# Attention with unnormalized weights, transposed reciprocals spread by GpSimd, and PSUM dealt out as four, three and one

## The chip, the core and the metric

One core of a Trainium2 chip. Five engines work side by side, each through its own queue in order: TensorE (PE; its weight loads are listed as PEld), VectorE (DVE), ScalarE (ACT), GpSimd (POOL) and SyncE (SP), which issues the DMAs. TensorE writes to PSUM alone, eight banks of 512 fp32 columns on 128 partitions; GpSimd cannot read PSUM. The metric is the device time of one execution in microseconds; less is better.

## The reference

Attention over 4 x 8 heads of 576 positions and 64 dimensions, with a rotation of q and k, and behind it two feed-forward layers on 2304 tokens of width 512 (inner width 2048):

```python
q_rot, k_rot = rotate(q), rotate(k)
scores = matmul(q_rot, k_rot.T) / sqrt(D)
attn = exp(scores - max(scores))
attn = attn / (sum(attn) + 1e-9)
x = matmul(attn, v)                       # -> (2304, 512)
h = x @ w_in;  x = where(h > 0, h, exp(min(h, 0)) - 1) @ w_out
h = x @ w2_in; x = (h - tanh(h)) @ w2_out
```

## The kernel before, in words

The 32 heads go in 16 pairs p. A pair is cut into nine items: four blocks u of 128 queries, each for head h = 0 and h = 1, and a last item (h is None) that holds the remaining 64 queries of both heads. Item i passes through a pipeline that one loop writes out by hand: in step i it emits, in this order, the maximum of item i (VectorE, `emit_max`), the copies out of PSUM that the last step left (`flush`, VectorE and ScalarE by a fixed turn), the scores of item i + 1 (`emit_s`), the exponential of item i with its sum (`emit_exp`, ScalarE), the reciprocal of item i - 1 and its multiplication into the weights (`emit_norm`, L235, VectorE and then GpSimd), the pieces of the rotation of later pairs that are due (`prep`), the transposes of item i - D (`emit_t`, D = 4), and the matmuls with v that are due (`emit_pv`, PV). The remainder of i by 9 is called the slot here. Each engine takes its work in this order.

Scores are made from split numbers: a rotated q or k is held as a rounded high half and a low half, and DMAs put the halves together (`place`, L167: four DMAs for a pair's k, two for each head, and four for q). `prep` has five pieces: two products with the table of cosines and sines, their sum, the high half (L147, ScalarE) and the low half (L152, VectorE), the latter followed by the DMAs. The k of pair p gets its high half in slot 3 and its low half in slot 4 of pair p - 1 (L328); pairs 1 and 2 have entries of their own. The scores of head 0 of pair p are emitted in slot 8 of pair p - 1, those of head 1 in slot 0.

The weights of two query blocks are transposed by TensorE (`pt`; the last 64 key columns of both heads go into `pr`), copied to SBUF (`aT`, `aTr`) and multiplied with v. The items of a group of two blocks are transposed, and L358 says how many steps later its five chunks follow: 12 matmuls after one step, 8 after three; the last group's 20 after two steps, together with the 8 of the second group. With D = 4 the PV stand in slots 3 (12 matmuls), 5 (28), 8 (12) and 1 (8). The result `o` is rounded to `xh` by ScalarE and the rest `xl` made by VectorE (L264 to L274). PSUM: two score tiles of two banks, two banks for transposes, two for outputs.

The feed-forward part works on blocks of 384 tokens, with `xh` and `xl` as its input and an accumulator `acc`; weights come as 64-bit words and are converted beside the rest (`conv_w`).

Of the kernel before, what the change touches and what calls it, by code (L numbers as in the profile page):

```python
# [23 lines left out]
def attention_elu_tanhshrink(ctx: ExitStack, tc: tile.TileContext, qk, v, w1i, w1o, w2i, w2o, tab, out):  # L24
# [22 lines left out]
    xh = const.tile([128, KC, NTOK], F32R, name="xh")  # L47
    xl = const.tile([128, KC, NTOK], F32R, name="xl")
# [52 lines left out]
    with ExitStack() as actx:  # L101
# [10 lines left out]
        tabs = acst.tile([128, 2, S], F32, name="tabs")  # L112
        zero = acst.tile([128, 64], F32, name="zero")
# [5 lines left out]
        def load_qk(p, x):  # L119
            if p == 1 and x == 0:  # L120
                t = p3.tile([128, 2, S], F32, tag="a", name="t0")
            else:
                t = (p1, p2)[x].tile([128, 2, S], F32, tag=f"t{x}", name=f"t{x}")
            nc.sync.dma_start(out=t, in_=qk[p, :, 2 * x:2 * x + 2, :])
            t_t[p, x] = t
# [6 lines left out]
        def prep(p, x, i):  # L132
            t = t_t[p, x]
            mul = SCALE if p > 0 and x == 0 else 1.0
            if i < 2:
                if p == 0 and x == 0:
                    nc.vector.scalar_tensor_tensor(
                        out=t[:, i, :], in0=t[:, i, :], scalar=SCALE, in1=tabs[:, i, :], op0=ALU.mult, op1=ALU.mult
                    )
                else:  # L140
                    eng = nc.vector if p < 2 and i == 1 else nc.gpsimd
                    eng.tensor_tensor(out=t[:, i, :], in0=t[:, i, :], in1=tabs[:, i, :], op=ALU.mult)  # L142
            elif i == 2:
                nc.vector.tensor_tensor(out=t[:, 0, :], in0=t[:, 0, :], in1=t[:, 1, :], op=ALU.add)  # L144
            elif i == 3:
                hl_t[p, x] = p1.tile([128, 2, S], F32R, tag=f"hl{x}", name=f"hl{x}")
                nc.scalar.mul(hl_t[p, x][:, 0, :], t[:, 0, :], mul)  # L147
# [87 lines left out]
        def emit_norm(i):  # L235
# [13 lines left out]

        ev = [0]  # L250
        late, late_x, late_l = [], [], []
# [4 lines left out]
        def flush():  # L256
            for out_, in_ in late:
                ev[0] += 1
                if ev[0] % 5 in (1, 3):
                    nc.vector.tensor_copy(out_, in_)  # L260
                else:
                    nc.scalar.copy(out_, in_)  # L262
            late.clear()
            for x0, hp, o, n in late_l:  # L264
                nc.vector.tensor_tensor(
                    out=xl[:, hp, x0:x0 + n], in0=o[:, 0:n], in1=xh[:, hp, x0:x0 + n].bitcast(F32),
                    op=ALU.subtract,
                )
            late_l.clear()
            for p, grp, o, n in late_x:  # L270
                b, hp = divmod(p, 4)
                x0 = b * S + 256 * grp
                nc.scalar.copy(out=xh[:, hp, x0:x0 + n], in_=o[:, 0:n])
                late_l.append((x0, hp, o, n))  # L274
            late_x.clear()

        def emit_t(i):
            p, u, h = items[i]
            a = a_t[p, u]
            grp = u // 2  # L280
            if (u % 2 == 0) and h in (0, None):
                if grp < 2:
                    aT_t[p, grp] = (p2.tile([128, 2, 4, 256], F32, tag="aT", name="aT"),
                                    p2.tile([128, 256], F32, tag="aTr", name="aTr"))
                else:
                    aT_t[p, grp] = (p1.tile([128, 2, 4, 64], F32, tag="aT2", name="aT2"),
                                    p1.tile([128, 64], F32, tag="aTr2", name="aTr2"))
            aT, aTr = aT_t[p, grp]
            q0 = 128 * (u % 2)
            pt = ps_t.tile([128, 4, 128], F32, tag="pt", name="pt")  # L290
            for c in range(4):
                c0 = 128 * c + (64 if h == 1 else 0)
                nc.tensor.transpose(pt[:, c, :], a[:, h or 0, c0:c0 + 128], ident)  # L293
            if h is None:
                for hh in range(2):
                    evac(aT[:, hh, :, 0:64], pt[:, :, 64 * hh:64 * hh + 64])
                pr = ps_t.tile([128, 4, 128], F32, tag="pt", name="pr")
                for hh in range(2):
                    sl = slice(64 * hh, 64 * hh + 64)
                    nc.tensor.matmul(out=pr[sl, 0, 0:64], lhsT=a[sl, 0, 512:576], rhs=ident[sl, sl],  # L300
                                     start=True, stop=True)
                evac(aTr[:, 0:64], pr[:, 0, 0:64])
                return
            evac(aT[:, h, :, q0:q0 + 128], pt)
            if h == 1:
                pr = ps_t.tile([128, 4, 128], F32, tag="pt", name="pr")
# [3 lines left out]
        o_t = {}  # L310

        def emit_pv(p, grp, c):
# [3 lines left out]
            if c == 0:  # L316
                o_t[p, grp] = ps_v.tile([128, 256], F32, tag="o", name="o")
            o = o_t[p, grp]
            for h in range(2):
                sl = slice(64 * h, 64 * h + 64)  # L320
                if c < 4:
                    w, m = vt[:, 128 * c + 64 * h:128 * c + 64 * h + 64], aT[:, h, c, 0:n]
                else:
                    w, m = vt[sl, 512:576], aTr[sl, 0:n]
# [4 lines left out]
            o_t.pop((p, grp))  # L329
            if grp == 2:  # L330
                v_t.pop(p)
            late_x.append((p, grp, o, n))

        D = 4
# [4 lines left out]
        early = {1: ((None, 0, 0, 1, 2, 3), (None, 0, 0, 0, 1, 2)), 2: ((2, 4, 5, 7, 7, 8), (4, 7, 9, 11, 12, 13))}  # L339
# [11 lines left out]
        with tc.manual_schedule():  # L351
            for x in range(2):
                t = t_t[0, x] = (p1, p2)[x].tile([128, 2, S], F32, tag=f"t{x}", name=f"t{x}")
# [5 lines left out]
            load_qk(1, 1)  # L359
            load_v(0)  # L360
# [10 lines left out]
            pend = []  # L371
            emit_s(0)
# [4 lines left out]
            for i in range(n + D + 1):  # L377
# [4 lines left out]
                if r == 0 and p % 2 == 0 and p // 2 < len(first_w):  # L382
                    load_w(first_w[p // 2])
# [7 lines left out]
                if 0 <= i - 1 < n:  # L391
                    emit_norm(i - 1)
# [20 lines left out]
            flush()  # L413
# [12 lines left out]
    acc = fcst.tile([128, KC * NTOK], F32, name="acc")  # L426
# [6 lines left out]
    def emit_f1(i):  # L433
# [4 lines left out]
        for c in range(KC):  # L438
            ws = slice(128 * c, 128 * c + 128)
            xs = slice(NB * t, NB * t + NB)  # L440
            for wp, x in ((0, xh), (0, xl), (1, xh)):
                nc.tensor.matmul(out=hp, lhsT=w[:, wp, ws], rhs=x[:, c, xs], start=(m == 0), stop=(m == 3 * KC - 1))  # L442
                m += 1
# [61 lines left out]
    def emit_acc():  # L505
        while y_done:
            l, g, t, ys = y_done.pop()
            for e, y in enumerate(ys):
# [11 lines left out]
                if l == 0:  # L520
                    xs = slice(NB * t, NB * t + NB)
                    nc.scalar.copy(out=xh[:, e, xs], in_=a)
                    nc.gpsimd.tensor_tensor(
                        out=xl[:, e, xs], in0=a, in1=xh[:, e, xs].bitcast(F32), op=ALU.subtract
                    )
# [7 lines left out]
    with tc.manual_schedule():  # L533
# [82 lines left out]
```

## Time and profile before

| | us |
|---|---|
| median of three runs (1137.78 to 1139.23) | 1138.52 |
| the profiled execution | 1137.68 |
| its span, first to last instruction | 1135.9 |
| TensorE busy | 1100.1 |
| VectorE, ScalarE, GpSimd busy | 769.7, 689.3, 647.6 |

The attention part takes the first 325 us. The busy time of TensorE counts overlapping matmuls once, and their ends are modelled: the time from one group's start to the next one's start tells its price better than its duration. An idle time stands in brackets with the engine and line that ended it.

### The profile page before, as it was taken

To read this page: it belongs to the slowest core of one execution; us is meant where nothing else is said; L and a number is where in the kernel's file an instruction comes from. 1 tells how busy PE (TensorE), PEld (TensorE's weight loads), DVE (VectorE), ACT (ScalarE), POOL (GpSimd) and SP (SyncE) were. 2 spreads that over 40 slices of the span, in tenths; PEclk is the share of its full clock that TensorE was granted. 3 is DMA by queue.
4 is the path that set the end of the run, shared out by engine and by line. 5 is a ranking of instruction groups with operands and counts; after the bars stand their busy time and mean duration, and the time that the engine had idled before them with its cause. 6 is when DMAs were issued, how large, how long until landed. Compare 5 with 4: busy or idle time off the path is not lost.

```text
span 1135.9 us, 18496 instructions
## 1 busy us (share of the span) xinstructions
PE 1100.1 (97%) x6656; PEld 983.9 (87%) x6656; DVE 769.7 (68%) x1383; ACT 689.3 (61%) x1479; POOL 647.6 (57%) x585
## 2 busy tenths in 40 slices
PE   2899999999999999999999999999999999999998
PEld 1677777777789999999999999999999999999997
DVE  5998889888743434455445466677768777877665
ACT  3677777777634343333333344688888788877774
POOL 2877888778423333333333366676666666666443
PEclk9999999999999999999999999999999999999999
DMA  7767676766211111111111111111111111110102
GB/s 231 197 193 192 191 182 189 200 195 187 72 38 38 38 38 40 54 38 38 57 38 38 38 50 44 38 38 38 56 38 38 38 55 39 38 38 1 57 34 79
DMA packets 29627, 91.96 MB, mean 81 GB/s; under 512 B 4192, under 2 KB 4192, under 8 KB 29536
## 3 DMA queue, kind: packets, MB, share of 16 engines
q1 hardware_dynamic: 29536, 90.78, 27.8%
q8 instruction: 53, 0.87, 0.3%
q14 instruction: 38, 0.31, 0.1%
HBM read 57.74 MB, written 4.72 MB: 55 GB/s over the span
## 4 chain that ended last, share of the span: by engine, by line
PE 86%; DVE 10%; DMA 2%; ACT 1%; issue 1%; SPq 1%; DVEq 0%; ACTq 0%
PE h L442 36%; PE y L498 18%; PE y L500 18%; PE o L325 6%; PE s L207 5%; PE pt L293 3%; DVE nm L216 3%; DVE aT L260 2%; DVE hl L152 1%; DMA k<-hl 1%; DVE den L242 1%; DVE t L144 1%; DVE f L79 1%; PE pr L307 1%; DMA tabs<-in_tab 0%
## 5 line engine op out<-in xcount | busy, mean ns | idle before, releaser
L442 PE MATMUL h<-xh,w 128*128 128x384 f32 x1536 | 423.3, 336 | 0.0
L483 POOL TENSOR_TENSOR g<-f,g 128x384 fp32r<-128x384 f32 x192 | 214.9, 1120 | 232.5 <-ACT g L482 229.2
L442 PEld LDWEIGHTS h<-xh,w 128*128 128x128 f32 x1536 | 281.6, 188 | 3.8
L442 PE MATMUL h<-xl,w 128*128 128x384 f32 x768 | 258.3, 336 | 0.0
L498 PE MATMUL y<-g,w 128*128 128x384 f32 x1152 | 219.0, 339 | 0.0
L500 PE MATMUL y<-w,g 128*128 128x512 f32 x864 | 216.5, 395 | 0.0
L498 PEld LDWEIGHTS y<-g,w 128*128 128x128 f32 x1152 | 204.0, 188 | 0.0
L500 PEld LDWEIGHTS y<-w,g 128*128 128x128 f32 x864 | 161.6, 188 | 31.4
L246 POOL TENSOR_SCALAR a<-a,r 128x576 f32<-128x576 f32 x144 | 132.4, 932 | 70.5 <-DVE r L243 50.4
L459 POOL TENSOR_TENSOR w<-w,u 128x384 f32<-128x384 f32 x96 | 105.9, 1103 | 100.1 <-ACT w L458 100.1
L482 ACT CAST g<-f 128x384 fp32r<-128x384 f32 x192 | 97.9, 510 | 99.4 <-PE y L498 97.7
L442 PEld LDWEIGHTS h<-xl,w 128*128 128x128 f32 x768 | 144.2, 188 | 3.8
L470 DVE TENSOR_SCALAR f<-f 128x384 f32<-128x384 f32 x96 | 38.4, 400 | 153.9 <-ACT f L451 153.9
L451 ACT ACTIVATE f<-h 128x384 f32<-128x384 f32 x96 | 47.2, 492 | 150.0 <-PE h L442 146.4
L230 ACT ACTIVATE a<-s,nm 128x576 f32<-128x576 f32 x144 | 107.6, 747 | 39.6 <-DVE nm L216 31.7
L216 DVE TENSOR_REDUCE nm<-s 128x1 f32<-128x576 f32 x144 | 108.1, 751 | 32.4 <-PE s L207 31.6
L96 POOL TENSOR_TENSOR w<-f,w 128x512 fp32r<-128x512 f32 x64 | 82.7, 1292 | 54.2 <-ACT w L95 54.1
L517 DVE TENSOR_TENSOR acc<-y,acc 128x384 f32<-128x384 f32 (+1 forms) x126 | 74.0, 612 | 47.2 <-PE y L498 42.0
L474 DVE TENSOR_TENSOR f<-h,f 128x384 f32<-128x384 f32 x96 | 53.2, 554 | 71.4 <-ACT f L460 70.9
L476 DVE COPY_PREDICATED f<-mask,w 128x384 f32<-128x384 uint32 x96 | 91.7, 956 | 10.3 <-ACT g L482 0.5
L142 POOL TENSOR_TENSOR t<-t,tabs 128x576 f32<-128x576 f32 x59 | 88.1, 1494 | 15.6 <-DMA t<-in_qk 15.6
L293 PE MATMUL pt<-ident,a 128*128 128x128 f32 x576 | 89.0, 277 | 4.0 <-ACT aT L262 2.7
(58 smaller groups left out, 1479.5 us busy)
## 6 DMA issues: line engine op xcount, KB each, us to landing
k<-hl SPq DMA_DIRECT2D x64, 288.0 KB, 4.6
t<-in_qk SPq DMA_DIRECT2D x30, 576.0 KB, 4.8
raw<-in_w1i SPq DMA_DIRECT2D x16, 512.0 KB, 3.7
raw<-in_w1o SPq DMA_DIRECT2D x16, 512.0 KB, 3.7
raw<-in_w2i SPq DMA_DIRECT2D x16, 512.0 KB, 3.6
raw<-in_w2o SPq DMA_DIRECT2D x16, 512.0 KB, 3.6
v<-in_v SPq DMA_DIRECT2D x16, 288.0 KB, 5.1
qa<-hl SPq DMA_DIRECT2D x32, 144.0 KB, 2.3
```

Of the source, the lines that this page charges most:

```text
L142: eng.tensor_tensor(out=t[:, i, :], in0=t[:, i, :], in1=tabs[:, i, :], op=ALU.mult)
L216: nc.vector.tensor_reduce(out=nm, in_=s_t[i][:, :, 0:288], axis=AX.XY, op=ALU.max, negate=True)
L230: nc.scalar.activation(out=a.rearrange("p (x c) -> p x c", x=2), in_=s[:, :, 0:288], func=AF.Exp, bias=nm_t.pop(i), scale=1.0, accum_out=den,)
L246: nc.gpsimd.tensor_scalar(out=a, in0=a, scalar1=r[:, x:x + 1], scalar2=1.0, op0=ALU.mult, op1=ALU.mult)
L293: nc.tensor.transpose(pt[:, c, :], a[:, h or 0, c0:c0 + 128], ident)
L442: nc.tensor.matmul(out=hp, lhsT=w[:, wp, ws], rhs=x[:, c, xs], start=(m == 0), stop=(m == 3 * KC - 1))
L459: nc.gpsimd.tensor_tensor(out=w, in0=w, in1=u, op=ALU.mult)
L476: nc.vector.copy_predicated(f, mask.bitcast(U32), w)
L482: nc.scalar.copy(out=g[:, 0, :], in_=f)
L483: nc.gpsimd.tensor_tensor(out=g[:, 1, :], in0=f, in1=g[:, 0, :].bitcast(F32), op=ALU.subtract)
L498: nc.tensor.matmul(out=y_t[e][:, 0:NB], lhsT=w[:, wp, es], rhs=gt[:, gp, :], start=st, stop=sp)
L500: nc.tensor.matmul(out=y_t[e], lhsT=gt[:, gp, es], rhs=w[:, wp, :], start=st, stop=sp)
```

## The change

The weights stay unnormalized. The reciprocal of a query's sum is spread by GpSimd over 128 columns (64 for each head), transposed by TensorE beside the last key columns, copied out with them, and multiplied into the output when VectorE takes it from PSUM. The output goes to SBUF as plain fp32 (`xa`, which also is the accumulator later); its split into high and low half is made for each 384 tokens (`split_x`), for the first block in the last items of attention, for the others in the first 20 steps of the feed-forward part. The scale 1/8 sits in a second table `tabq`, made by GpSimd. The low halves of q and k of pairs 1 to 15 are made by GpSimd. 1e-9 is added column by column. Transposes get three banks and outputs one, which the second and third group of a pair share. D is 3. Loads of q and of the first weights are issued at other steps.

```diff
-    xh = const.tile([128, KC, NTOK], F32R, name="xh")
-    xl = const.tile([128, KC, NTOK], F32R, name="xl")
+    xa = const.tile([128, KC * NTOK], F32, name="xa")
+    x_t = {0: const.tile([128, 2, KC, NB], F32R, name="x0")}
+    def split_x(t, c):
+        a = xa[:, NTOK * c + NB * t:NTOK * c + NB * t + NB]
+        x = x_t[t]
+        nc.scalar.copy(out=x[:, 0, c, :], in_=a)
+        nc.gpsimd.tensor_tensor(out=x[:, 1, c, :], in0=a, in1=x[:, 0, c, :].bitcast(F32), op=ALU.subtract)
...
-        ps_t = actx.enter_context(tc.tile_pool(name="ps_t", bufs=2, space=PSUM))
-        ps_v = actx.enter_context(tc.tile_pool(name="ps_v", bufs=2, space=PSUM))
+        ps_t = actx.enter_context(tc.tile_pool(name="ps_t", bufs=3, space=PSUM))
+        ps_v = actx.enter_context(tc.tile_pool(name="ps_v", bufs=1, space=PSUM))
...
-                nc.vector.scalar_tensor_tensor(
-                    out=hl[:, 1, :], in0=t[:, 0, :], scalar=mul, in1=hl[:, 0, :].bitcast(F32),
-                    op0=ALU.mult, op1=ALU.subtract,
+                eng = nc.vector if p == 0 else nc.gpsimd
+                eng.tensor_tensor(
+                    out=hl[:, 1, :], in0=t[:, 0, :], in1=hl[:, 0, :].bitcast(F32), op=ALU.subtract
                 )
...
-            nc.vector.tensor_scalar_add(den, den, 1e-9)
+            rs = r_t[p, u] = sm.tile([128, 128], F32, tag="rs", name="rs")
+            for x in range(nh):
+                nc.vector.tensor_scalar_add(den[:, x:x + 1], den[:, x:x + 1], 1e-9)
             nc.vector.reciprocal(out=r[:, 0:nh], in_=den)
-            for x in range(nh):
-                a = a_t[p, u][:, x, :]
-                nc.gpsimd.tensor_scalar(
-                    out=a, in0=a, scalar1=r[:, x:x + 1], scalar2=1.0, op0=ALU.mult, op1=ALU.mult
-                )
+            nc.gpsimd.tensor_copy(
+                rs.rearrange("p (h d) -> p h d", h=nh), r[:, 0:nh].unsqueeze(2).broadcast_to([128, nh, 128 // nh])
+            )
...
+        def flush_o():
+            for p, grp, o, aTr, n in late_o:
                 b, hp = divmod(p, 4)
-                x0 = b * S + 256 * grp
-                nc.scalar.copy(out=xh[:, hp, x0:x0 + n], in_=o[:, 0:n])
-                late_l.append((x0, hp, o, n))
-            late_x.clear()
+                x0 = NTOK * hp + b * S + 256 * grp
+                for sl, r in ((slice(0, 128), aTr[:, 1, :]),) if grp < 2 else (
+                        (slice(0, 64), aTr[0:64, 0, 64:128]), (slice(64, 128), aTr[64:128, 0, 128:192])):
+                    nc.vector.tensor_tensor(out=xa[sl, x0:x0 + n], in0=o[sl, 0:n], in1=r, op=ALU.mult)
+            late_o.clear()
...
-                nc.tensor.transpose(pr[:, 0, :], a.rearrange("p h s -> p (h s)")[:, 512:640], ident)
-                evac(aTr[:, q0:q0 + 128], pr[:, 0, :])
+                nc.tensor.transpose(pr[:, 0:128], a.rearrange("p h s -> p (h s)")[:, 512:640], ident)
+                nc.tensor.transpose(pr[:, 128:256], r_t.pop((p, u)), ident)
+                evac(aTr[:, :, q0:q0 + 128], pr[:, 0:256].rearrange("p (x c) -> p x c", x=2))
...
-        D = 4
+        D = 3
...
-                when = [i0 + o for o in ((-8, -6, -4, -3, -2, -1), (-7, -2, 0, 2, 3, 4))[x]]
+                when = [i0 + o for o in ((-10, -6, -4, -3, -2, -1), (-7, -2, 0, 2, 3, 4))[x]]
...
+            nc.gpsimd.tensor_scalar(out=tabq, in0=tabs, scalar1=SCALE, scalar2=1.0, op0=ALU.mult, op1=ALU.mult)
             load_v(0)
             make_identity(nc, ident)
...
-                    emit_norm(i - 1)
+                    emit_recip(i - 1)
+                flush_o()
...
+                if n - 8 <= i < n and (i - n) % 2 == 0:
+                    split_x(0, (i - n + 8) // 2)
...
+            if i < NJ * (NT - 1):
+                split_x(i // NJ + 1, i % NJ)
```

## Rows read from the trace of the kernel before

**Rows 1.** Busy us (and instructions) by stretch: PE, PEld, DVE, ACT, POOL; clock, DMA share, GB/s.
```profile
36.00:325.00 289.00, 280.08 (x2287) 205.83 (x2285) 247.48 (x519) 202.27 (x504) 215.62 (x201) 1.00 0.63 171
325.00:700.00 375.00, 375.00 (x2132) 375.00 (x2131) 183.04 (x361) 137.15 (x276) 145.47 (x130) 1.00 0.14 43
```
**Rows 2.** Waits, 36 to 325 us: waiter and releaser, us in total, times, longest.
```profile
PEld pr L307 <- DVE aT L260: 8.4, 15, 0.9
...
PEld s L207 <- ACT a L230: 3.7, 21, 0.2
PE pt L293 <- ACT aT L262: 2.7, 7, 0.7
...
PEld s L207 <- ACT aT L262: 2.7, 7, 0.4
```
**Rows 3.** TensorE in order of time: start us, us, group; from slot 4 on.
```profile
158.47 0.80 PE L207 MATMUL s<-k,qb 128*128 128x288 f32 x4
159.10 0.60 PE L293 MATMUL pt<-ident,a 128*128 128x128 f32 x4
159.46 0.77 PE L207 MATMUL s<-k,qa 128*128 128x288 f32 x4
...
161.17 0.33 PE L307 MATMUL pr<-ident,a 128*128 128x128 f32 x1 [0.51 <-DVE aT L260]
...
163.47 0.80 PE L207 MATMUL s<-k,qb 128*128 128x288 f32 x4
...
164.59 0.80 PE L207 MATMUL s<-k,qa 128*128 128x288 f32 x4
...
165.85 0.66 PE L293 MATMUL pt<-ident,a 128*128 128x128 f32 x4
166.34 0.27 PE L307 MATMUL pr<-ident,a 128*128 128x128 f32 x1
166.37 0.77 PE L207 MATMUL s<-k,qa 128*128 128x288 f32 x4
167.28 0.63 PE L293 MATMUL pt<-ident,a 128*128 128x128 f32 x4
...
169.28 0.80 PE L207 MATMUL s<-k,qb 128*128 128x288 f32 x4
```
**Rows 4.** Groups of one shape, 20 to 300 us: busy us, mean ns, idle before.
```profile
L246 POOL TENSOR_SCALAR a<-a,r 128x576 f32<-128x576 f32 x135 | 125.8, 945 | 61.2 <-DVE r L243 41.1 <-PE s L207 10.1 <-PE o L325 2.5
L230 ACT ACTIVATE a<-s,nm 128x576 f32<-128x576 f32 x135 | 100.8, 747 | 33.9 <-DVE nm L216 26.0 <-DVE den L242 7.8
L142 POOL TENSOR_TENSOR t<-t,tabs 128x576 f32<-128x576 f32 x56 | 83.0, 1482 | 8.3 <-DMA t<-in_qk 8.3
...
L260 DVE COPY aT<-pt 128x512 f32<-128x512 f32 x44 | 29.9, 680 | 0.1
...
L242 DVE TENSOR_SCALAR den<-den 128x1 f32<-128x1 f32 x15 | 2.2, 144 | 0.0
```
**Rows 5.** VectorE and GpSimd in order of time: start us, us, group.
```profile
159.09 0.76 DVE L152 SCALAR_TENSOR_TENSOR hl<-t,hl 128x576 fp32r<-128x576 f32 x1
...
162.62 0.17 DVE L243 RECIPROCAL r<-den 128x2 f32<-128x2 f32 x1
162.98 1.81 POOL L246 TENSOR_SCALAR a<-a,r 128x576 f32<-128x576 f32 x2 [0.42 <-DVE r L243]
164.30 0.76 DVE L216 TENSOR_REDUCE nm<-s 128x1 f32<-128x576 f32 x1 [0.85 <-PE s L207]
```
**Rows 6.** DMAs of k: four issued from 140.97; then the last two of another pair.
```profile
DMA to landing us min/median/max: 3.0/4.5/5.4
...
L174 SPq DMA_DIRECT2D k<-hl x2: 863/1100/1338, 161.1 to 162.0; - x2
DMA to landing us min/median/max: 4.8/5.8/6.7
```
**Rows 7.** GpSimd at the start, in order of time.
```profile
7.95 1.40 POOL L142 TENSOR_TENSOR t<-t,tabs 128x576 f32<-128x576 f32 x1 [6.64 <-DMA t<-in_qk]
```

More of the change, by code (lines that the diff above doesn't have):

```diff
@@ L107, in attention_elu_tanhshrink @@
         ps_s = actx.enter_context(tc.tile_pool(name="ps_s", bufs=2, space=PSUM))
-        ps_t = actx.enter_context(tc.tile_pool(name="ps_t", bufs=2, space=PSUM))
-        ps_v = actx.enter_context(tc.tile_pool(name="ps_v", bufs=2, space=PSUM))
+        ps_t = actx.enter_context(tc.tile_pool(name="ps_t", bufs=3, space=PSUM))
+        ps_v = actx.enter_context(tc.tile_pool(name="ps_v", bufs=1, space=PSUM))
         ident = acst.tile([128, 128], F32, name="ident")
         tabs = acst.tile([128, 2, S], F32, name="tabs")
+        tabq = acst.tile([128, 2, S], F32, name="tabq")
         zero = acst.tile([128, 64], F32, name="zero")
@@ L119, in load_qk @@
         def load_qk(p, x):
[L120 to L123, printed above, removed]
+            t = p2.tile([128, 2, S], F32, tag=f"t{x}", name=f"t{x}")
             nc.sync.dma_start(out=t, in_=qk[p, :, 2 * x:2 * x + 2, :])
@@ L133, in prep @@
             t = t_t[p, x]
-            mul = SCALE if p > 0 and x == 0 else 1.0
             if i < 2:
@@ L146, in prep @@
                 hl_t[p, x] = p1.tile([128, 2, S], F32R, tag=f"hl{x}", name=f"hl{x}")
-                nc.scalar.mul(hl_t[p, x][:, 0, :], t[:, 0, :], mul)
+                nc.scalar.copy(out=hl_t[p, x][:, 0, :], in_=t[:, 0, :])
             else:
@@ L233, in emit_exp, with emit_recip @@
             )
-        def emit_norm(i):
+        def emit_recip(i):
             p, u, h = items[i]
@@ L241, in emit_norm @@
             r = sm.tile([128, 2], F32, tag="r", name="r")
[L242 removed]
+            rs = r_t[p, u] = sm.tile([128, 128], F32, tag="rs", name="rs")
+            for x in range(nh):
+                nc.vector.tensor_scalar_add(den[:, x:x + 1], den[:, x:x + 1], 1e-9)
             nc.vector.reciprocal(out=r[:, 0:nh], in_=den)
[L244 to L248 removed]
+            nc.gpsimd.tensor_copy(
+                rs.rearrange("p (h d) -> p h d", h=nh), r[:, 0:nh].unsqueeze(2).broadcast_to([128, nh, 128 // nh])
+            )
+        r_t = {}
         ev = [0]
[L251 removed]
+        late, late_o = [], []
         def evac(out_, in_):
@@ L283, in emit_t @@
                     aT_t[p, grp] = (p2.tile([128, 2, 4, 256], F32, tag="aT", name="aT"),
-                                    p2.tile([128, 256], F32, tag="aTr", name="aTr"))
+                                    p2.tile([128, 2, 256], F32, tag="aTr", name="aTr"))
                 else:
                     aT_t[p, grp] = (p1.tile([128, 2, 4, 64], F32, tag="aT2", name="aT2"),
-                                    p1.tile([128, 64], F32, tag="aTr2", name="aTr2"))
+                                    p1.tile([128, 1, 192], F32, tag="aTr2", name="aTr2"))
             aT, aTr = aT_t[p, grp]
@@ L296, in emit_t @@
                     evac(aT[:, hh, :, 0:64], pt[:, :, 64 * hh:64 * hh + 64])
-                pr = ps_t.tile([128, 4, 128], F32, tag="pt", name="pr")
+                pr = ps_t.tile([128, 512], F32, tag="pt", name="pr")
                 for hh in range(2):
                     sl = slice(64 * hh, 64 * hh + 64)
-                    nc.tensor.matmul(out=pr[sl, 0, 0:64], lhsT=a[sl, 0, 512:576], rhs=ident[sl, sl],
+                    nc.tensor.matmul(out=pr[sl, 0:64], lhsT=a[sl, 0, 512:576], rhs=ident[sl, sl],
                                      start=True, stop=True)
-                evac(aTr[:, 0:64], pr[:, 0, 0:64])
+                nc.tensor.transpose(pr[:, 64:192], r_t.pop((p, u)), ident)
+                evac(aTr[:, 0, :], pr[:, 0:192])
                 return
@@ L305, in emit_t @@
             if h == 1:
-                pr = ps_t.tile([128, 4, 128], F32, tag="pt", name="pr")
-                nc.tensor.transpose(pr[:, 0, :], a.rearrange("p h s -> p (h s)")[:, 512:640], ident)
-                evac(aTr[:, q0:q0 + 128], pr[:, 0, :])
-        o_t = {}
+                pr = ps_t.tile([128, 512], F32, tag="pt", name="pr")
+                nc.tensor.transpose(pr[:, 0:128], a.rearrange("p h s -> p (h s)")[:, 512:640], ident)
+                nc.tensor.transpose(pr[:, 128:256], r_t.pop((p, u)), ident)
+                evac(aTr[:, :, q0:q0 + 128], pr[:, 0:256].rearrange("p (x c) -> p x c", x=2))
+        o_t, second = {}, []
         def emit_pv(p, grp, c):
@@ L315, in emit_pv @@
             vt = v_t[p]
-            if c == 0:
-                o_t[p, grp] = ps_v.tile([128, 256], F32, tag="o", name="o")
-            o = o_t[p, grp]
+            if c == 0 and grp < 2:
+                o_t[p, grp] = ps_v.tile([128, 512], F32, tag="o", name="o")
+            o = o_t[p, min(grp, 1)][:, 256 * (grp == 2):256 * (grp == 2) + n]
             for h in range(2):
@@ L328, in emit_pv @@
             aT_t.pop((p, grp))
-            o_t.pop((p, grp))
+            done = (p, grp, o, aTr, n)
+            if grp == 1:
+                second.append(done)
+                return
             if grp == 2:
                 v_t.pop(p)
-            late_x.append((p, grp, o, n))
-        D = 4
+                late_o.append(second.pop())
+            o_t.pop((p, min(grp, 1)))
+            late_o.append(done)
+        D = 3
         NDIRECT = 2
@@ L338, in attention_elu_tanhshrink @@
         sched = {}
-        early = {1: ((None, 0, 0, 1, 2, 3), (None, 0, 0, 0, 1, 2)), 2: ((2, 4, 5, 7, 7, 8), (4, 7, 9, 11, 12, 13))}
+        early = {1: ((None, 0, 0, 1, 2, 3), (None, 0, 0, 0, 1, 2)), 2: ((0, 4, 5, 7, 7, 8), (4, 7, 9, 11, 12, 13))}
         for p in range(1, NPAIR):
@@ L352, in attention_elu_tanhshrink @@
             for x in range(2):
-                t = t_t[0, x] = (p1, p2)[x].tile([128, 2, S], F32, tag=f"t{x}", name=f"t{x}")
+                t = t_t[0, x] = p2.tile([128, 2, S], F32, tag=f"t{x}", name=f"t{x}")
                 for i in range(2):
@@ L371, in attention_elu_tanhshrink @@
             pend = []
+            nw = list(range(len(first_w)))[::-1]
             emit_s(0)
@@ L381, in attention_elu_tanhshrink @@
                         f(*arg)
-                if r == 0 and p % 2 == 0 and p // 2 < len(first_w):
-                    load_w(first_w[p // 2])
+                if i == 1 or i % (2 * NI) == 12:
+                    load_w(first_w[nw.pop()]) if nw else None
                 if i < n:
@@ L424, in attention_elu_tanhshrink @@
     ps_y = ctx.enter_context(tc.tile_pool(name="ps_y", bufs=4, space=PSUM))
-    acc = fcst.tile([128, KC * NTOK], F32, name="acc")
+    for t in range(1, NT):
+        x_t[t] = fcst.tile([128, 2, KC, NB], F32R, name=f"x{t}")
+    acc = xa
     b1 = fcst.tile([128, 1], F32, name="b1")
@@ L439, in emit_f1 @@
             ws = slice(128 * c, 128 * c + 128)
-            xs = slice(NB * t, NB * t + NB)
-            for wp, x in ((0, xh), (0, xl), (1, xh)):
-                nc.tensor.matmul(out=hp, lhsT=w[:, wp, ws], rhs=x[:, c, xs], start=(m == 0), stop=(m == 3 * KC - 1))
+            for wp, xp in ((0, 0), (0, 1), (1, 0)):
+                nc.tensor.matmul(
+                    out=hp, lhsT=w[:, wp, ws], rhs=x_t[t][:, xp, c, :], start=(m == 0), stop=(m == 3 * KC - 1)
+                )
                 m += 1
@@ L520, in emit_acc @@
                 if l == 0:
[L521 to L525, printed above, removed]
+                    split_x(t, e)
                 else:
```

14 lines of the change are left out of this document (4 added, 10 removed).

## The prediction

> **What bounds the kernel now.** I read the busy time by stretch first: the reader is to see that in the feed-forward part TensorE is busy for all of 375 us, and in the attention part for 280.1 of 289 [rows 1]. So nothing can be won behind 325 us, and in front of it TensorE's own work nearly sets the pace. Second, the waits: the reader is to see what TensorE's loads and matmuls stand for between 36 and 325 us. Waits for the copies that empty the transposes' banks make 8.4 + 2.7 + 2.7 = 13.8 us, and waits for an exponential, which frees a score buffer, 3.7 us [rows 2]. Third, TensorE in order of time over about one pair, for the price of each group of matmuls and for the places of the output groups (PV): they stand in slots 3, 5, 8 and 1 [rows 3]. Last, the DMAs of the rotated k: how long behind VectorE's last product they land, and how long before the score that reads them.
>
> The sum is made against the profiled execution: span 1135.9 us, 1137.68 with what lies around it, 0.84 under the median of 1138.52.
>
> **The change part by part**
>
> Added on TensorE: 80 transposes of the spread reciprocals, 64 beside the transpose of the last key columns and 16 in the last item of a pair. Four transposes and the start of the fifth lie 0.49 us apart [rows 3], so one is 0.12. The 64 cost 7.7; the 16 stand between products on 64 rows and a PV, where nothing runs ahead, and I take the 0.27 us that a lone one lasts [rows 3]: 4.3. Together 12. Bounds: 80 x 0.03 = 2.4, if each fits into the hand-over to the next score (166.34 to 166.37), and 80 x 0.27 = 22.
>
> The Trainium skill, "TensorE: Matmul & The Clock Gate", Part 4, gives about 275 ns to a transpose in a kernel's context and says that the fast clock does not engage for it. The granted clock in the rows is 1.00, the level of 2.4 GHz, through the whole attention part [rows 1], so the trace disagrees on the clock; by 275 ns each the 80 would cost 22 us and the total would be some 10 us above my forecast.
>
> Gone on TensorE: a third bank for transposes. An item with two transpose tiles is now followed by one that still finds a free bank, whose emptying has a whole step. I take all 13.8 us (bounds 0 and, with the 3.7 for score buffers, 17.5). One bank for the outputs costs nothing: the next PV that reuses it stands two steps behind the multiply that empties it, a score and a transpose group at least.
>
> VectorE and GpSimd: GpSimd loses 144 multiplies of 0.945 us [rows 4] and gets 80 spreads of 128 columns, 30 subtractions for the low halves, and one scaling of the table. VectorE loses those 30 subtractions, the 48 for the low half of the output and, by adding 1e-9 column by column (0.144 us [rows 4]), waits; it gets 64 multiplies. ScalarE loses 48 casts. None of the three is a sum on the path: what counts is where an operation stands in its queue.
>
> Moved, and this decides: the lag goes from 4 to 3 steps, so each PV stands one step earlier: 28 matmuls in slot 4 instead of 5, 12 in slot 2 and slot 7 instead of 3 and 8, 8 in slot 0. The schedule of the k product does not move with it: its low half is still made in slot 4, now by GpSimd, behind the spread of the reciprocals. Before, it ended at 159.85 [rows 5], 1.38 us behind the start of slot 4 at 158.47, because the long PV of slot 3 had let VectorE run ahead. After, slot 3 holds a score and a transpose, 0.99 us (158.47 to 159.46 shows such a step [rows 3]). From its start: the maximum begins 0.83 behind the score's start (163.47 to 164.30) and lasts 0.76 [rows 3, 5]; that is 0.60 behind the start of slot 4. Then the copy aT 0.68 [rows 4], two additions of 0.144 [rows 4] and a reciprocal of 0.17, 0.19 to the start on GpSimd (162.79 to 162.98 [rows 5]), the spread, and the product 1.48 [rows 4]. For the spread no row has this form; bounds are 0.144, the smallest operation on 128 rows, and 0.945, the multiply of 576 columns [rows 4]; 128 columns are nearer the small one and I take 0.30. The sum is 0.60 + 0.68 + 0.29 + 0.17 + 0.19 + 0.30 + 1.48 = 3.71 us behind the start of slot 4, 2.3 later than before.
>
> Behind it SP issues four k DMAs (and holds the v load and the q DMAs, which have a pair of slack). The last one is issued 2.1 us behind the product's end (162.0 - 159.85) and lands 5.4 us later in one pair, 6.7 in another [rows 6]: 7.5 or 8.8 us behind the product. The second head's first score, slot 0 of the next pair, reads it. Before it began at 169.28, 10.81 behind the start of slot 4 [rows 3], with 1.9 or 0.6 us to spare. After, slot 4 is score 0.63, transposes 0.49 and 0.12, last transpose with PV 2.30 = 3.54; slot 5 is 0.99; slots 6 and 8 are 0.63 + 0.49 + 0.12 + 0.03 = 1.27 each; slot 7 is the long score 1.26 and transpose with PV 2.00 (167.28 to 169.28) = 3.26 [rows 3]. Together 10.33, and 0.16 more to the second matmul, which reads the last part: 10.5. The k arrives at 3.71 + 7.5 = 11.2 or 3.71 + 8.8 = 12.5. TensorE waits 0.7 or 2.0 us. With two pairs to go by, I weigh the early landing, whose four DMAs have a median of 4.5 us [rows 6], two to one: 1.13 us a pair, times 14 pairs (2 to 15 follow the regular schedule) = 15.8. The waits for score buffers, 3.7 us, go, since TensorE is now held elsewhere. Bounds: 0, if the product comes 0.7 us earlier than I think, and 14 x 2.0 = 28, or 37 with the dear spread.
>
> Start: the table's scaling runs ahead of the first k product on GpSimd, which began at 7.95 [rows 7]. Two halves of 576 columns at 0.945 are 1.9 if nothing hides it, 0 if the table is there long before the k; I take 1.2. Its wait for the table's DMA also holds the identity behind it, needed only by the first transpose. End: the splits of the first 384 tokens run beside the last scores, the other 20 on ScalarE and GpSimd under a full TensorE [rows 1]; without that cover each costs about a step, but the first is wanted only after 48 matmuls.
>
> Sum: 12 - 13.8 + 15.8 - 3.7 + 1.2 = 11.5 us in the profile. The two middle terms rest on means over a few pairs, and I round the sum down to 10: 1147.7, in the median's terms 1148.
>
> **The rivals**
>
> Faster: the k product is in time. GpSimd has no more multiplies before it, VectorE no waits for it; if the product ends 0.7 us earlier, or the DMAs land early because the q and v loads moved, the term of 15.8 is gone. Then 12 - 13.8 - 3.7 + 1.2 = -4.3, so 1134 in the median's terms; at most, with the transposes wholly in hand-overs, -14: 1124. For it: 15 waits for the banks by name [rows 2]. Against it: the slack of 0.6 us in the late pair, against 2.3 us of delay. It decides at a landing 10.5 us behind the start of slot 4.
>
> No change: k in time, but score buffers bind. Behind the PV of 28 two short steps now follow (0.99 + 1.27 = 2.26 us) before the long score, which needs the exponential of the first: 0.83 + 0.76 + 0.75 + hand-overs, about 2.6 [rows 4, 5]. That is 0.35 us in 15 pairs, 5 us, in place of the 3.7: 12 - 13.8 + 5 - 3.7 + 1.2 = 0.7, so 1139. Against it: VectorE is also free to run ahead there.
>
> The spread is dear: at 0.945 it delays every k by 0.65, 14 x 0.65 = 9 more: 1157. The Trainium skill, "SBUF — State Buffer", section "Who interferes with whom", says that a VectorE instruction with two SBUF inputs contends with a GpSimd instruction that reads SBUF; moving the low halves to GpSimd puts k under that rule. The product of 1.48 in the sum is already a mean with such waits, and 0.75 more a pair by the rule would give this same 1157.
>
> **How the numbers follow.** The k wait 0.45, the dear spread 0.07, no change 0.17, faster 0.31. A measurement of this kernel can tell 0.2% (2.3 us) from no change: the band is 1136.2 to 1140.8. Of the no-change case 0.14 falls into it, 0.02 above and 0.01 below; of the k case 0.02 falls into it. Faster 0.32, within 0.2% 0.16, slower 0.52. The range reaches from 1131, in the faster case, to 1157; the likeliest case's own is 1141 (0.5 us of k wait a pair) to 1156 (1.6).
>
> **What would show it.** After the change the waits should list scores for the k DMA some 14 times with 0.5 to 2 us each, waits for the copies should fall under 3 us, and the k product should end about 3.7 us behind the start of slot 4. No wait for k, or an attention part that ends before 325 us, makes the forecast wrong; a spread over 0.6 us or added transposes over 0.2 us apart make its terms wrong.

## The result: slower by 0.7%, and the profile after the change

The changed kernel takes 1146.53 us (median of 4 runs, 1145.44 to 1147.64), the kernel before on the same chip 1138.54 (4 runs); the ratio is 1.0070, 95% interval 1.0053 to 1.0088. The profiled execution took 1147.64 us, its span 1145.9, 10.0 longer than before. By the starts of the scores 1.6 of that lies ahead of pair 2, 9.5 in the 13 pairs from 2 to 14, and 1.1 is won behind them.

Busy time by stretch after the change (columns as in [rows 1]):

```profile
36.00:330.00 294.00, 280.56 (x2316) 211.70 (x2316) 216.35 (x561) 191.51 (x460) 162.47 (x171) 1.00 0.63 169
330.00:700.00 370.00, 370.00 (x2125) 368.73 (x2122) 186.73 (x357) 142.72 (x291) 160.65 (x146) 1.00 0.14 42
```
The feed-forward part is as full as before. In the attention part TensorE is idle for 13.4 us in place of 8.9 [rows 1], although VectorE and GpSimd have less to do.

The waits after the change, 36 to 335 us (as [rows 2]):

```profile
PEld s L212 <- ACT a L235: 18.1, 30, 1.4
...
PE s L212 <- ACT a L235: 10.2, 15, 1.2
...
PEld s L212 <- ACT aTr L268: 3.1, 4, 1.0
PEld s L212 <- ACT aT L268: 2.7, 7, 0.4
...
PE s L212 <- DMA k<-hl: 0.8, 1, 0.8
```
The 8.4 us for aT [rows 2] are gone, as forecast; the 2.7 us of scores waiting for aT on ScalarE, which the prediction added to them, stand as before. Scores wait for exponentials, that is for score buffers: their weight loads 18.1 us in place of 3.7 (the row of PE counts the longer of the same stops again, from the matmul's side). A wait for k is named once; of the four loads that wait for aTr, three are those of the second head's first score, which reads the late k.

One pair with an even number, TensorE, VectorE, ScalarE and GpSimd from slot 3 on (as [rows 3, 5]):

```profile
180.50 0.80 PE L212 MATMUL s<-k,qa 128*128 128x288 f32 x4
181.14 0.60 PE L296 MATMUL pt<-ident,a 128*128 128x128 f32 x4
...
181.34 0.76 DVE L221 TENSOR_REDUCE nm<-s 128x1 f32<-128x576 f32 x1 [0.96 <-PE s L212]
...
181.79 0.80 PE L212 MATMUL s<-k,qb 128*128 128x288 f32 x4
...
182.43 0.60 PE L296 MATMUL pt<-ident,a 128*128 128x128 f32 x4
...
182.86 0.27 PE L311 MATMUL pr<-ident,a 128*128 128x128 f32 x1
...
182.97 0.27 PE L312 MATMUL pr<-ident,rs 128*128 128x128 f32 x1
...
183.15 0.29 POOL L251 COPY rs<-r 128x128 f32<-128x128 f32 x1 [2.26 <-PE pr L311]
...
183.40 1.41 POOL L158 TENSOR_TENSOR hl<-t,hl 128x576 fp32r<-128x576 f32 x1
...
185.21 0.80 PE L212 MATMUL s<-k,qa 128*128 128x288 f32 x4
...
185.33 0.79 DVE L277 TENSOR_TENSOR xa<-o,aTr 128x256 f32<-128x256 f32 x3 [1.33 <-PE o L331]
...
186.15 0.43 DVE L85 TENSOR_SCALAR f<-f 128x512 f32<-128x512 f32 x1
...
186.20 0.77 PE L212 MATMUL s<-k,qb 128*128 128x288 f32 x4
...
186.61 0.43 DVE L86 TENSOR_SCALAR f<-f 128x512 uint32<-128x512 uint32 x1
...
187.07 0.76 DVE L221 TENSOR_REDUCE nm<-s 128x1 f32<-128x576 f32 x1
...
187.92 0.74 ACT L235 ACTIVATE a<-s,nm 128x576 f32<-128x576 f32 x1 [0.85 <-DVE den L249]
...
188.81 0.80 PE L212 MATMUL s<-k,qa 128*128 128x288 f32 x4 [1.17 <-ACT a L235]
```
VectorE idles 1.33 us for the long PV, then makes the output multiplies and, in even pairs, two operations of the weight conversion (L85, L86); only then comes the maximum (187.07) of item 6, whose score began at 185.21, ahead of the multiplies. Its exponential (187.92) frees the buffer for the long score of the pair's last item, 188.81. In an odd pair the conversion is not there, and the maximum follows the multiplies at once:

```profile
166.05 0.79 DVE L277 TENSOR_TENSOR xa<-o,aTr 128x256 f32<-128x256 f32 x3 [1.32 <-PE o L331]
...
166.87 0.76 DVE L221 TENSOR_REDUCE nm<-s 128x1 f32<-128x576 f32 x1
```

The table is worked out from the traces: mean us from the start of the score issued in a slot to the start of the next score, pairs 2 to 14 (even and odd rows: 3 to 14, where the last column adds the rounded slots). The experiments below are listed in it by their labels.

```
slot                  8    0    1    2    3    4    5    6    7   pair
before             3.00 1.10 2.41 1.28 2.95 0.99 3.83 1.15 1.78  18.48
after              1.44 2.29 1.21 3.10 1.29 3.42 0.99 2.18 3.29  19.21
  even pairs       1.43 2.29 1.21 3.10 1.29 3.42 0.99 2.60 3.29  19.62
  odd pairs        1.31 2.30 1.21 3.10 1.29 3.42 1.00 1.68 3.29  18.60
a_k_early          1.21 2.30 1.21 3.24 1.21 3.42 1.00 2.17 3.29  19.05
a_no_rt            1.45 2.30 1.15 2.85 1.59 3.31 0.99 2.18 3.29  19.11
a_out_act          1.57 2.30 1.21 3.10 1.28 3.42 1.00 1.85 3.31  19.04
a_mul_later        1.92 2.32 1.21 3.10 1.28 3.42 1.00 1.86 3.42  19.52
a_pv_split         1.87 2.31 1.21 3.10 1.28 2.55 2.04 1.53 3.36  19.25
a_pv_spread        2.46 1.74 1.21 2.68 1.75 2.54 2.04 1.32 3.13  18.86
a_conv, even       1.24 2.30 1.21 3.10 1.28 3.42 1.00 1.73 3.38  18.66
a_conv, odd        1.80 2.30 1.24 3.11 1.94 3.42 0.99 1.68 3.29  19.77
a_lag4             2.63 1.21 2.30 1.20 3.33 1.06 3.41 1.00 2.89  19.03
a_banks_old        1.36 2.47 1.21 3.26 1.13 3.52 0.99 2.18 3.29  19.40
b_banks            2.66 1.33 2.31 1.27 2.87 0.99 3.29 1.62 1.78  18.13
a_three            2.82 1.08 2.30 1.12 2.85 0.99 3.29 0.99 1.87  17.31
```

### The profile page after: what moved, and what is told of

Read it like the earlier page. It is cut to its first block, busy times and chain, and to the rows that moved or that the text cites. A ratio compares the mean times of both kernels' runs of the same rounds, so it can differ in the third digit from the quotient of the medians.

```text
span 1145.9 us, 18650 instructions
## 1 busy us (share of the span) xinstructions
PE 1105.8 (97%) x6736; PEld 993.6 (87%) x6736; DVE 747.6 (65%) x1433; ACT 687.5 (60%) x1455; POOL 616.1 (54%) x576
## 4 chain that ended last, share of the span: by engine, by line
PE 85%; DVE 5%; DMA 5%; ACT 3%; SPq 1%; issue 1%; POOL 0%; ACTq 0%; POOLq 0%
PE h L459 35%; PE y L517 18%; PE y L519 17%; PE o L331 6%; PE s L212 6%; PE pt L296 3%; DMA t<-in_qk 2%; ACT a L235 2%; DVE nm L221 2%; DMA k<-hl 1%; DVE aT L266 1%; DVE t L149 1%; DVE xa L277 0%; DMA v<-in_v 0%; ACT aTr L268 0%
## 5 line engine op out<-in xcount | busy, mean ns | idle before, releaser
L459 PE MATMUL h<-x,w 128*128 128x384 f32 x2304 | 433.8, 336 | 0.0
L459 PEld LDWEIGHTS h<-x,w 128*128 128x128 f32 x2304 | 407.2, 188 | 7.6
L251 POOL COPY rs<-r 128x128 f32<-128x128 f32 x80 | 36.3, 454 | 131.7 <-DVE r L250 89.7
L536 DVE TENSOR_TENSOR xa<-y,xa 128x384 f32<-128x384 f32 (+1 forms) x126 | 74.0, 612 | 47.2 <-PE y L517 42.0
L475 ACT ACTIVATE u<-h 128x384 f32<-128x384 f32 x96 | 47.4, 494 | 67.2 <-PE h L459 52.0
L268 ACT COPY aT<-pt 128x512 f32<-128x512 f32 x96 | 52.8, 550 | 51.4 <-PE pt L296 31.1
L212 PE MATMUL s<-k,qa 128*128 128x288 f32 x316 | 64.1, 325 | 16.9 <-ACT a L235 11.7
```

Of the source, the lines that this page charges most:

```text
L212: nc.tensor.matmul(out=s[:, half, o0:o0 + n], lhsT=w, rhs=k[:, part, c0:c0 + n], start=(m == 0 and part == 0), stop=(m == len(terms) - 1 a ...
L459: nc.tensor.matmul(out=hp, lhsT=w[:, wp, ws], rhs=x_t[t][:, xp, c, :], start=(m == 0), stop=(m == 3 * KC - 1))
```

## The experiments

Labels with a_ start from the changed kernel, with b_ from the kernel before. Each ratio is against the kernel before on the same chip, with its 95% interval; the changed kernel's own is 1.0070 (1.0053 to 1.0088). The late-k theory is the prediction's: TensorE waits for k. The queue theory came from the trace above: the score of slot 7 waits for its buffer, because the maximum of item 6 stands on VectorE behind multiplies that wait for the long PV. The differences of about 1 us between single runs and the changed kernel lie within the intervals; the slots of the table show more.

**a_k_early.** k one step earlier, in the list of steps (it and the list `PV_AT` stand in L343 and L373 of the kernel before, not in L328 and L358).
```diff
-                when = [i0 + o for o in ((-10, -6, -4, -3, -2, -1), (-7, -2, 0, 2, 3, 4))[x]]
+                when = [i0 + o for o in ((-10, -6, -4, -3, -2, -1), (-7, -2, 0, 1, 2, 3))[x]]
```


> The changed kernel (1146.5 us) with the k of the next pair finished one step earlier: sum, high half and low half in slots 1, 2, 3 in place of 2, 3, 4. Late-k theory (the prediction's): TensorE waits 1.1 us in each of 14 pairs for k, so 12 to 16 us come back: 1131 to 1135. Queue theory (from the trace after the change: 16.6 us of waits for score buffers in 13 pairs, 3.0 for k): at most the k waits come back, 0 to 4 us: 1142.5 to 1146.5, with the waits for score buffers as they were or longer.

Measured: 1145.79 us, ratio 1.0066 (1.0053 to 1.0078). Slot 8, where the score waits for k, falls from 1.44 to 1.21; the waits for score buffers stay:
```profile
PEld s L212 <- ACT a L235: 17.1, 30, 1.4
...
PE s L212 <- ACT a L235: 10.1, 15, 1.2
```
Late k is not the main cause. Slot 2 gives 0.14 of it back.

**a_mul_later.** The output multiplies one step later.
```diff
-                flush_o()
+                if r != 5:
+                    flush_o()
```


> The changed kernel with the output multiplies behind the long PV issued one step later (slot 6 in place of 5), so that the maximum of item 6 stands ahead of them on VectorE. Queue theory: the long score in slot 7 waits 0.96 us in the mean because that maximum stands behind multiplies that wait for the PV; its wait falls to 0.35 to 0.5, 6 to 9 us in all: 1138 to 1141. Late-k theory: k is not touched; time won in slot 7 turns into a wait for k in slot 0: 1145 to 1147.

Measured: 1151.73 us, ratio 1.0116 (1.0100 to 1.0131): slower, which neither theory had. VectorE and GpSimd of an even pair:
```profile
186.11 1.41 POOL L158 TENSOR_TENSOR hl<-t,hl 128x576 fp32r<-128x576 f32 x1
...
186.63 1.17 DVE L85 TENSOR_SCALAR f<-f 128x512 f32<-128x512 f32 x1
...
187.47 1.60 POOL L147 TENSOR_TENSOR t<-t,tabq 128x576 f32<-128x576 f32 x1
...
187.84 1.52 DVE L86 TENSOR_SCALAR f<-f 128x512 uint32<-128x512 uint32 x1
...
189.28 0.74 DVE L221 TENSOR_REDUCE nm<-s 128x1 f32<-128x576 f32 x1
...
190.26 0.77 DVE L277 TENSOR_TENSOR xa<-o,aTr 128x256 f32<-128x256 f32 x3
...
190.72 1.41 POOL L147 TENSOR_TENSOR t<-t,tabs 128x576 f32<-128x576 f32 x1
...
191.06 1.69 DVE L149 TENSOR_TENSOR t<-t 128x576 f32<-128x576 f32 x1
...
192.78 0.76 DVE L221 TENSOR_REDUCE nm<-s 128x1 f32<-128x576 f32 x1
```
The conversion, no longer behind the multiplies, meets GpSimd's products and takes 1.17 + 1.52 us in place of 0.43 + 0.43. That does not make the kernel slower by itself: even pairs, which alone hold these two operations, take 19.58 us in place of 19.62, odd pairs 19.22 in place of 18.60. In pairs of both kinds the multiplies now stand right ahead of an addition (L149), which runs into a GpSimd product, takes 1.7 us in place of 0.76 and holds the next maximum; by the rows that is the likely cause, not tested by itself. The wait in slot 6 shrinks by 0.32 a pair and comes back in slots 8 (+0.48) and 7 (+0.13).

**a_lag4.** The lag back at 4 steps: `D = 4`.

> The changed kernel with the lag of the transposes back at 4 steps, so that the PV groups stand in slots 3, 5, 8 and 1 as before. Queue theory: the long PV and its multiplies stand one step later, the maximum of item 6 is ahead of them; waits for score buffers fall from 16.6 to about 5 us in 13 pairs and those for k from 3 to 0: 8 to 13 us less, 1133 to 1138. Late-k theory: k gets back its slack and nothing else changes: 12 to 16 us less, 1131 to 1135, with the waits for score buffers at 4 us or less. The waits in its trace tell the two apart.

Measured: 1144.64 us, ratio 1.0057 (1.0045 to 1.0070): less than a quarter of the least that either theory said. The waits for k and in slot 6 are gone, but now the first score of the next pair waits behind slot 7 (2.89 where a_three has 1.87). TensorE, VectorE and GpSimd of an even pair:
```profile
185.54 0.77 DVE L277 TENSOR_TENSOR xa<-o,aTr 128x256 f32<-128x256 f32 x3
...
186.00 1.43 POOL L147 TENSOR_TENSOR t<-t,tabs 128x576 f32<-128x576 f32 x1
...
186.34 1.71 DVE L149 TENSOR_TENSOR t<-t 128x576 f32<-128x576 f32 x1
...
188.08 0.76 DVE L221 TENSOR_REDUCE nm<-s 128x1 f32<-128x576 f32 x1
...
189.75 0.80 PE L212 MATMUL s<-k,qa 128*128 128x288 f32 x4 [1.36 <-ACT a L235]
```
Behind the multiplies an addition runs into a GpSimd product (1.71 in place of 0.76), the maximum waits behind both. That happens in even pairs alone: their slot 7 takes 3.26 us in the mean, that of the odd ones 2.41.

**a_no_rt.** No transposes of the reciprocals.
```diff
-nc.tensor.transpose(pr[:, 128:256], r_t.pop((p, u)), ident)
-evac(aTr[:, :, q0:q0 + 128], pr[:, 0:256].rearrange("p (x c) -> p x c", x=2))
+r_t.pop((p, u))
+evac(aTr[:, :, q0:q0 + 128], pr[:, 0:128].unsqueeze(1).broadcast_to([128, 2, 128]))
```
(and the like in the last item of a pair; the output is left unscaled.)

> The changed kernel without the 80 transposes of the reciprocals: the copy out of the bank reads the transposed weights once more in their place, so the output is not scaled by the reciprocals; everything else stays. Queue theory: 0.11 us for 64 and 0.26 us for 16 of them, 11 us on TensorE; in slots 5 to 7 a part of it turns into a longer wait for score buffers: 6 to 11 us less, 1135.5 to 1140.5. Late-k theory: between the long PV and the score that waits for k they only fill time before k lands; 2 to 6 us less, 1140.5 to 1144.5, with the waits for k longer by as much.

Measured: 1145.68 us, ratio 1.0061 (1.0048 to 1.0073), 0.85 less than the changed kernel, below both expectations. The table shows where 80 transposes went: slots 1 and 2 win 0.31 us a pair and slot 3 gives 0.30 back; slots 6 and 8 win nothing, since TensorE waits there; only slot 4 keeps its 0.11. (In the profile pair 2 begins 1.7 us later than in the changed kernel, which hides a part of the gain; why is open.) Slot 3 in the trace of this kernel: from the transposes to the next score 1.01 us, where the changed one took 0.65 (181.14 to 181.79):
```profile
181.53 0.60 PE L296 MATMUL pt<-ident,a 128*128 128x128 f32 x4
...
182.54 0.80 PE L212 MATMUL s<-k,qb 128*128 128x288 f32 x4 [0.41 <-ACT a L235]
```

**b_banks.** In the kernel before: `ps_t` 3, `ps_v` 1, the second and third output group of a pair in one bank.

> The kernel before with the new deal of banks alone: three for transposes, one for outputs (the outputs of a pair's second and third group share it), weights scaled as before, no reciprocals transposed, lag 4. Bank theory (the prediction's term): the 13.8 us of waits for copies out of the transposes' banks go and nothing takes their place: 1123 to 1127. Given-back theory: TensorE does not bound the short slots, the score path through VectorE and ScalarE does; the waits only change their name to score buffers: 1134 to 1139.

Measured: 1131.80 us, ratio 0.9947 (0.9935 to 0.9960): between the two. The score waits of this kernel, 36 to 335 us:
```profile
PEld s L207 <- ACT a L230: 16.1, 38, 1.3
...
PE s L207 <- ACT a L230: 7.6, 21, 0.9
```
By the table, slots 8, 2, 3 and 5, where TensorE stood for copies, win 1.06 us a pair; slots 6 and 0 give 0.70 back as waits for exponentials (16.1 us in place of 3.7 [rows 2]). It is faster than both kernels of the case.

**a_banks_old.** The changed kernel with `ps_t` 2 and `ps_v` 2.

> The changed kernel with the old deal of banks, two for transposes and two for outputs, all else as changed. If the deal is worth here what it was worth alone in the kernel before (6.7 us): 1151 to 1155. If the waits for the transposes' copies that it takes away come back in full (13.8 us): 1158 to 1162. If VectorE and ScalarE hold TensorE anyway, whatever the banks: 1145 to 1149.

Measured: 1153.62 us (1150.52 to 1155.74), ratio 1.0127 (1.0109 to 1.0146). By the medians the deal is worth 7.1 us here too, as alone (by the profiled executions, 1150.52 and 1147.64, 2.9). The deal is the good part of the change.

**a_out_act.** The output copied out by ScalarE.
```diff
-nc.vector.tensor_tensor(out=xa[sl, x0:x0 + n], in0=o[sl, 0:n], in1=r, op=ALU.mult)
+nc.scalar.copy(out=xa[sl, x0:x0 + n], in_=o[sl, 0:n])
```


> The changed kernel with the output taken out of its bank by a copy on ScalarE in the same place in the program, in place of VectorE's multiply by the transposed reciprocals, so that the output is left unscaled. Queue theory, VectorE's order: the maximum of item 6 no longer stands behind multiplies that wait for the long PV, the long score's 0.99 us of wait a pair goes down to 0.3 or less: 7 to 13 us less, 1133 to 1139. Rival: the wait in slot 7 has another releaser (the conversion, the copies, ScalarE's own queue) and the copies on ScalarE hold the exponentials instead: within 3 us of 1146.5.

Measured: 1145.65 us, ratio 1.0069 (1.0056 to 1.0081): within the rival's 3 us. VectorE's order does hold the long score, but it is worth less than the queue theory said: slot 6 wins 0.33 us a pair, slot 8, with k, gives 0.13 back.

**a_pv_split.** `PV_AT[2] = (3, 3, 3, 3, 3)`: the third group one step later.

> The changed kernel with the third output group (20 matmuls, 0.95 us) one step later: slot 4 then holds 8 output matmuls and slot 5 holds 20, in place of 28 and none. TensorE's work is the same. Queue theory: a long PV gives VectorE and ScalarE nothing to do and the short slots behind it are too short for them; spread out, the score waits of 0.99 us in slot 7 fall to 0.5 or less: 5 to 9 us less, 1137 to 1141. If TensorE's own work or k set the pace: within 2 us of 1146.5.

Measured: 1150.33 us, ratio 1.0110 (1.0093 to 1.0127): a miss. Slot 6 falls by 0.65, slots 4 and 5 together grow by 0.18, slot 8 by 0.43: the wait moved. Of the profiled execution's 2.5 us more, 1.7 lie ahead of pair 2; the cause of these stays open.

**a_pv_spread.** `PV_AT = ((1, 1, 2, 2, 3), (1, 1, 2, 3, 3), (3, 3, 3, 3, 3))`.

> The changed kernel with the output groups dealt over seven slots: 8 matmuls each in slots 7, 8 and 2, 4 in slots 0 and 3, 8 in slot 4 and the 20 of the third group in slot 5, in place of 12, 28, 12 and 8 in four slots. Queue theory: no slot is far longer than the score path through VectorE and ScalarE needs and few are shorter; of 1.5 us of score and k waits a pair, 0.5 to 1.2 go: 7 to 17 us less, 1129 to 1139. If TensorE's own work sets the pace: within 2 us of 1146.5; if each more change between output group and score costs TensorE time (three more a pair): up to 5 us more.

Measured: 1141.72 us, ratio 1.0039 (1.0025 to 1.0052): 4.8 less than the changed kernel, less than expected. Slots 8, 3 and 5, which got a group, grow by 2.53 us a pair; the others shrink by 2.87, of which 0.86 is slot 6's wait. Without that the steps have grown by 0.52: the cost that the last branch of the expectation names, though what is won is larger than it.

**a_conv.** The conversion four steps later: `c = NI * (p % 2) + r - 7`, the load at `i % (2 * NI) == 14`.

> The changed kernel with the weight conversion four steps later: its three VectorE parts in slots 0, 2 and 4 of an odd pair, in place of slots 5 and 7 of an even pair and 0 of an odd one (the load of the next raw weights two steps later, behind their last use). Conversion theory (from the steps of the pairs: an even pair of the changed kernel takes 19.62 us, an odd one 18.60, and the whole difference is in slot 6, where the long score waits 1.42 or 0.49 us; in slot 5 of an even pair two conversion operations stand on VectorE behind multiplies that wait for the long output group, and ahead of the maximum): even pairs come to about 18.6, 7 to 8 us less, 1138.5 to 1140. Rival, the wait only moves, as in the two runs that moved multiplies and output groups: odd pairs get longer by as much, 1144 to 1148.

Measured: 1149.98 us, ratio 1.0087 (1.0073 to 1.0101). Even pairs come to 18.66, as the theory said; odd pairs go from 18.60 to 19.77, as the rival said (slot 8 +0.49, slot 3 +0.65). Two pairs take 38.43 us in place of 38.22, and the start of pair 2 lies 3.7 us later: that is where this run lost against the changed kernel (3.5 us by the medians), and why is open. At lag 3 the conversion costs about 1 us in every second pair, in either place.

**a_lag4_conv.** The same at lag 4, offset 8, load at 15.

> The same with the lag back at 4 steps: output groups in slots 3, 5, 8 and 1, the conversion five steps later, its VectorE parts in slots 1, 3 and 5 of an odd pair. Conversion theory: at lag 4 an even pair took 19.63 us and an odd one 18.21; even pairs come to 18.2 to 18.4, 9 to 11 us less than with lag 4 alone (1144.6): 1134 to 1136, faster than the kernel before in spite of its 80 transposes more. Rival, the wait only moves: odd pairs get longer by as much, 1142 to 1147.

Measured: 1142.26 us, ratio 1.0029 (1.0017 to 1.0040): 2.4 less than lag 4 alone. Even pairs 18.82, odd 18.77, in place of 19.63 and 18.21: most of it has moved.

**a_three.** a_lag4, a_no_rt and a_out_act in one.

> The changed kernel with three of the earlier edits at once: lag 4, no transposes of the reciprocals, and the outputs copied by ScalarE (so the output is left unscaled). Alone they gave 1.9, 0.85 and 0.9 us, 3.6 in sum. Substitution theory: each of them shortens one of several chains that end within a few tenths of a us of each other (TensorE's own work, the score path with the multiplies and the conversion on VectorE), so each alone is given back as a wait on another; together they give most of the 14.7 us by which the kernel before with the new banks (1131.8) is faster than the changed kernel: 1131 to 1136. Additive theory: 1142 to 1144.5, and the rest of the 14.7 lies in what is left of the change (the low halves on GpSimd, the spread, the start and the splits in the feed-forward part).

Measured: 1120.25 us, ratio 0.9837 (0.9823 to 0.9850): 26.3 us less than the changed kernel, where the three alone gave 3.6 in sum. The additive theory falls; the substitution theory was right in kind and too timid, since b_banks, from which its size came, waits itself. Busy time in 56 to 300 us, first the changed kernel, then this one:
```profile
56.00:300.00 244.00, 233.30 (x1929) 176.23 (x1926) 181.88 (x467) 159.12 (x382) 140.93 (x145) 1.00 0.67 178
```
```profile
56.00:300.00 244.00, 241.45 (x2060) 186.41 (x2059) 191.00 (x462) 187.69 (x480) 150.41 (x158) 1.00 0.69 186
```
TensorE idles 2.6 us in place of 10.7, with 131 matmuls more in the same time. What remains of waits of scores for exponentials in 36 to 335 us:
```profile
PEld s L212 <- ACT a L235: 4.0, 10, 0.6
```

## Why the prediction was right, and where it was wrong

The time was right: 1148 forecast, 1146.53 measured, on the side that had the largest chance. The reason that carried it was not, so the nearness of the time is luck: two terms were wrong by 12 to 16 us each, with opposite signs. The prediction's own sign of its reason, some 14 waits for k by name, came out as one.

A hand-over below is the time from the start of a group's last matmul to the start of the next group's first.

- **Transposes, +12: right in size on TensorE.** They lie 0.11 us apart (182.86 to 182.97); over 13 pairs they add 9.0 us, 11.1 for 16 pairs. One record lasts 0.27 us, near the 275 ns that the Trainium skill ("TensorE: Matmul & The Clock Gate", Part 4) gives to a transpose in a kernel's context; what an added one costs behind another is the 0.11 us, at a granted clock of 1.00. But that their whole price stands on the path was wrong: taking them away alone (a_no_rt) gave 0.85 us.
- **Copies out of the transposes' banks, -13.8: right as waits** (-13.9 in 13 pairs, by the starts of the matmuls). That the size agrees is in part luck, since one of the three rows added up for it, 2.7 us, is still there. That nothing takes their place was wrong: alone the deal gives 6.7 us, the rest comes back as waits for score buffers.
- **Late k, +15.8: the step that failed first.** The product ends 3.02 us behind the start of slot 4 (183.40 + 1.41 - 181.79), not 3.71: the maximum ahead of it began 0.45 ahead of slot 4 instead of 0.16, because slot 3 lasts 1.29 us and not 0.99 (the score of slot 4 waits for its buffer), the additions and the product are a little shorter, and the spread takes 0.29, as forecast. That is the 0.7 us at which the prediction let the term go. The score that reads k also comes later than forecast, 11.3 us behind the start of slot 4 in the mean (slots 4 to 8 of the table) in place of 10.3, 0.9 of it by slot 6. So waits for score buffers stand where the wait for k was to stand; how much k alone would cost without them is open. What is left is slot 8, 1.44 against 1.21: 3 us in 13 pairs, 4.0 with the last, most of it in four pairs and not in 14. Taking it away gives 0.7 us (a_k_early), within the intervals.
- **Waits for score buffers, -3.7: wrong in sign.** "TensorE is now held elsewhere" failed; against the shortest hand-over of each kind these waits rise from 4.4 to 16.6 us in the 13 pairs. The rival that gave no change had the mechanism and priced it at 0.35 us a pair. Odd pairs wait 0.49 in slot 6; even pairs 1.42, because the rival's chain left out what stands ahead of the maximum on VectorE: multiplies that wait for the long PV, and the conversion behind them.
- **Start, +1.2: right on GpSimd, not told apart in the time.** The first product on GpSimd begins at 9.21 in place of 7.95 [rows 7], the first score 0.56 us later, pair 2 1.6 us later; the last holds the transposes and waits of the first pairs too. The splits cost nothing that shows.
- **The sum.** 9.0 for transposes, -13.9 for copies, +12.2 for score buffers, +3.0 for k and -0.8 in smaller hand-overs make the 9.5 of the 13 pairs.

What the sum could not hold is that its terms are not additive. Score path, k and TensorE's own work ended within some tenths of a us of each other where TensorE waits; shortening one lengthened the wait for the next. Shown: each of three edits alone is worth 2 us or less, together 26.3. At lag 4 without multiplies on VectorE and without the transposes TensorE nearly sets the pace, 17.31 us a pair. Between a_lag4 and a_three the 13 pairs get 22.4 us shorter: the waits above the shortest hand-overs fall from 15.8 to 5.1, and the rest is TensorE's own work, the 9.0 of the transposes among it. Open: which of the two edits, at lag 4, is worth how much; the table puts 1.02 of 1.72 us into slot 7 (the score wait behind the multiplies) and 0.48 into slot 3, but no two of the three edits were run together. Nor did a run move the low halves back from GpSimd, or leave the weights unnormalized, by itself. (a_three leaves work out and shows only where the time is; of the kernels that do all the work b_banks is the fastest.)

## What to carry to other kernels

Where a chain runs through three engines with two buffers, a term of a sum counts only until the next chain takes over: work out when every chain ends in each slot, and try edits in combination before one is called worthless. Moving an operation that waits for a long matmul group onto an engine that also stands in the path that frees the buffers puts that wait ahead of everything queued there. Compare steps of even and odd rounds: what runs in every second round shows itself at once.

## What the runs showed of the hardware that was not expected

VectorE and GpSimd held each other up even in VectorE operations with one input: L85 and L86 took 0.43 us each in the changed kernel and 1.17 and 1.52 beside GpSimd's products in a_mul_later, one of which took 1.60 where the others took 1.41 to 1.43; L149, two inputs, took 0.76 and, in a_lag4 and a_mul_later, 1.69 to 1.71; the maximum, which reads PSUM, stayed at 0.74 to 0.76. The Trainium skill, "SBUF — State Buffer", section "Who interferes with whom", says of VectorE's 2-port modes that the one that issues first gets the shared pair of ports for its whole instruction. No row shows in which mode an operation ran, but the rows fit such a lock: each stretched operation shown begins while a GpSimd product runs and is done 0.28 to 0.62 us after that product has ended. The prediction weighed that section's rule on two inputs for the k product, where it made no difference; it bore on the conversion and the additions.
